# Moving GpSimd's subtractions to VectorE in a fused attention and two-MLP kernel, and pinning one more weight chunk in VectorE's order

## The chip, the cores and the metric

The kernel runs on one core of a Trainium2 chip. The metric is the device time of one execution in microseconds. Three runs of the kernel before gave 616.75 us (median), 614.03 and 618.17.

## The reference

Causal attention over 2 batches, 12 heads, 448 positions and a head size of 64 gives 896 tokens of width 768. They go through two MLPs, all in fp32:

```
x = attention(q, k, v)                       # softmax, masked above the diagonal
h = x @ w_in;  g = 0 | (h+1)^2/4 | h         # 768 -> 2048, piecewise
y = g @ w_out                                # 2048 -> 768
u = silu(y @ w_gate) * (y @ w_val)           # 768 -> 1536, twice
out = u @ w_out2                             # 1536 -> 768
```

## The kernel before, in words

**Splitting.** TensorE reads operands rounded to `fp32r`. Each fp32 operand x is therefore split into a high part (a rounded copy, made by ScalarE) and a low part (x minus the high part, a subtraction). Each product is three matmuls: high times high, high times low, low times high (`mm3`, L83 to L86, and `add`, L717). A low part of weights is named `wl` (L212), `vl` (L256, half of a chunk of `val`) or `ol` (L244, the last projection); of y it is `yl`, of the sums of y `tl` (both L96). The high parts are `wh`, `vh`, `oh`, `yh`, `th`.

**Narrowing.** The weights come from HBM as raw 64-bit words (`wraw`) and are made into 32-bit floats (`wt`) by three VectorE instructions each, `narrow`: L102, L105, L108. A second, independent chain narrows other weights ahead of time in small pieces (`araw`, `at`) and stores them to HBM (`n<-at`, a DMA issued on ScalarE's queue, L140); they come back later as `wraw<-n`.

**Stages.** Attention for both halves of the tokens, with the first products of h beside it (to 146 us); the rest of h (to 231); y, six column blocks d of three weight pieces each, 96 matmuls a block (231 to 350.5); gate and val, twelve chunks f; the last projection, 21 groups of 18 matmuls (534.6 on). Chunks 0, 1, 10 and 11 use `eight`: eight products of 9 matmuls, 72 in all. Chunks 2 to 9 use `seven`: Strassen-like sums of y (`T1` to `T4`, raw form `traw`) and of the weights (`ws`, split into `sh` and `sl`) save one product of eight, 63 matmuls a chunk. There ScalarE copies partial results out of PSUM (`one`, `two`, `three`, `five`, L745 to L758) before TensorE may add to the same bank again.

**Buffers.** Weight halves stand in `WBUFS = 4` rotating buffers, so the split of weight i waits until TensorE has used weight i - 4. Raw words have two buffers, narrowed words (`wt`) two.

**Order.** The Tile layer places each engine's instructions by its own plan of times and priorities; at run time every engine works strictly in that order and waits where an operand is missing. In `narrowing`, a flag `pin` calls `tc.keep_in_program_order` on the first instruction, so that the planner may not bring it ahead of what stands before it in the program. `PIN0, PIN1` bound the weights of gate and val for which the flag is set: numbers 0 and 1 are gate and val of chunk 0, 2 and 3 those of chunk 1.

**The splits of y** stand in the program behind the last block of y: twelve `yh`/`yl` pairs (two token halves g, six blocks c; `yl0_3` is g = 0, c = 3), then the last three `traw`, then four `th`/`tl`. The first product of chunk 0 needs `yl0_0`, the sixteenth matmul `yh0_5`, the 37th `yh1_0`.

Of the kernel before, what the change touches and what calls it, by code (L numbers as in the profile page):

```python
# [8 lines left out]
F32 = mybir.dt.float32  # L9
# [4 lines left out]
ALU = mybir.AluOpType  # L14
# [13 lines left out]
HALF = DM // 2  # L28
# [7 lines left out]
EARLY = WBUFS + STAY  # L36
MASK = -1.0e9 * 8.0
BF16 = mybir.dt.bfloat16
LOW_V = 9
NORM_P = 0  # L40
TURN0 = "A"
TURN1 = "A"
# [1 line left out]
NORM1 = "V"  # L44
SEVEN = (2, 3, 4, 5, 6, 7, 8, 9)
TICK8 = (1, 2)
PIN0, PIN1 = 4, 28
APART = (3, 4, 6, 8, 9)
PART, PART_BUFS = 384, 2
TERMS = (("Z11", "W11"), ("Z21", "W12"), ("T1", "S1"), ("T2", "S2"), ("Z22", "S4"), ("T3", "S3"), ("T4", "W22"))  # L50
# [16 lines left out]
def fused_kernel(ctx: ExitStack, tc: tile.TileContext, qk, v, w_in, w_out, w_gv, w_o2, out):  # L67
    nc = tc.nc
# [74 lines left out]
    class Weights:  # L143
# [36 lines left out]
        def operations(self):  # L180
            for at, (kind, i, src, n) in enumerate(self.seq):
# [20 lines left out]
                if f in SEVEN and i < I_O2:  # L202
# [8 lines left out]
                nc.scalar.copy(out=wh[:, :n], in_=t)  # L211
                (nc.vector if i < LOW_V else nc.gpsimd).tensor_tensor(  # L212
                    out=wl[:, :n], in0=t, in1=wh[:, :n].bitcast(F32), op=ALU.subtract,
# [5 lines left out]
        def term(self, at, i):  # L219

            k, p = divmod(i - I_O2, OUT_PAIRS)
            name = TERMS[k][1]
            if k < 2:
                t = quads[0].tile([128, WB], I32, name=f"{name}_{p}")
                yield from self.narrowing(at, self.raw.pop(("op", i)), t, False)
                quad[name, p] = t.bitcast(F32)
            elif k == 2 and p == 0:
                for q in range(OUT_PAIRS):
                    for low in ("W21", "W22"):
                        quad[low, q] = quads[1].tile([128, WB], F32, name=f"{low}_{q}")  # L230
                        nc.sync.dma_start(out=quad[low, q], in_=stored[low, q])
            made = {
                "S1": ("W21", "W22", "W21", ALU.add), "S2": ("S1", "W11", "S1", ALU.subtract),
                "S4": ("W12", "S2", "W12", ALU.subtract), "S3": ("W22", "S2", "W11", ALU.subtract),
            }
            if name in made:
                a, b, home, op = made[name]
                nc.vector.tensor_tensor(out=quad[home, p], in0=quad[a, p], in1=quad[b, p], op=op)
                quad[name, p] = quad[home, p]
                yield  # L240
            wh = wp.tile([128, WB], F32R, tag="wh", name="oh")
            wl = wp.tile([128, WB], F32R, tag="wl", name="ol")
            nc.scalar.copy(out=wh, in_=quad[name, p])
            (nc.vector if k else nc.gpsimd).tensor_tensor(  # L244
                out=wl, in0=quad[name, p], in1=wh.bitcast(F32), op=ALU.subtract)
            self.got[i] = wh, wl
            self.ready = i + 1
            yield

        def sums(self, i, gate, val):  # L250

            g, v = ([x[:, k * HALF:(k + 1) * HALF] for k in range(2)] for x in (gate, val))
            wh = wp.tile([128, WB], F32R, tag="wh", name="vh")
            wl = wp.tile([128, WB], F32R, tag="wl", name="vl")
            nc.scalar.copy(out=wh[:, :HALF], in_=v[1])
            nc.gpsimd.tensor_tensor(out=wl[:, :HALF], in0=v[1], in1=wh[:, :HALF].bitcast(F32), op=ALU.subtract)  # L256
            t = sums_p.tile([128, 4 * HALF], F32, tag="s", name="ws", bufs=1)
            sh = sums_p.tile([128, 3 * HALF], F32R, tag="sh", name="sh")
            sl = sums_p.tile([128, 3 * HALF], F32R, tag="sl", name="sl")
            s1, s2, s3, s4 = (t[:, k * HALF:(k + 1) * HALF] for k in range(4))  # L260
            nc.vector.tensor_tensor(out=s1, in0=v[0], in1=v[1], op=ALU.add)
            nc.vector.tensor_tensor(out=s2, in0=s1, in1=g[0], op=ALU.subtract)
            yield
            nc.vector.tensor_tensor(out=s4, in0=g[1], in1=s2, op=ALU.subtract)
            nc.vector.tensor_tensor(out=s3, in0=g[0], in1=v[0], op=ALU.subtract)
            yield
            for hi, lo, x in ((sh[:, :WB], sl[:, :WB], t[:, :WB]), (sh[:, WB:], sl[:, WB:], s3),
                              (wh[:, HALF:], wl[:, HALF:], s4)):
                nc.scalar.copy(out=hi, in_=x)
                (nc.vector if S_LOW == "V" else nc.gpsimd).tensor_tensor(  # L270
                    out=lo, in0=x, in1=hi.bitcast(F32), op=ALU.subtract)
                if x is not s4:
                    yield
            self.got[i] = wh, wl, sh, sl
            self.ready = i + 1
            yield
# [25 lines left out]
    for i, (src, n) in enumerate(srcs):  # L302
# [3 lines left out]
        if i >= I_O2:  # L306
            k, p = divmod(i - I_O2, OUT_PAIRS)
# [61 lines left out]
    with ExitStack() as ph:  # L369
# [158 lines left out]
        def zeros(n):  # L528
# [10 lines left out]
            out=mask_b[:C, :], in_=mask_b[:C, :], compare_op=ALU.is_ge, fill=MASK,  # L539
# [115 lines left out]
    for d in range(KC):  # L655
        pss = [bank() for _ in range(2)]
        for i, (a, b) in enumerate(OUT_CUTS):
            wi = I_Y + 3 * d + i
            wh, wl = W.get(wi)
# [78 lines left out]
    def seven(f, ws):  # L738
# [10 lines left out]
        nc.vector.tensor_tensor(out=b, in0=b, in1=one, op=ALU.add)  # L749
        W.tick(1)  # L750
        add(a, sums, HALF, sums_of(1), False, True)
        nc.scalar.copy(out=two, in_=a)
        W.tick(1)
        add(c, sums, 0, sums_of(0), True, True)
        nc.scalar.copy(out=five, in_=c)
        W.tick(1)
        add(a, sums, 2 * HALF, sums_of(2), False, True)
        nc.scalar.copy(out=three, in_=a)  # L758
        W.tick(1)
# [71 lines left out]
    for k in range(len(TERMS)):  # L831
# [3 lines left out]
        for p in range(OUT_PAIRS):  # L835
# [6 lines left out]
            for c in range(6):  # L842
                sl = slice(c * 128, (c + 1) * 128)
                for e, (a, b) in enumerate(((0, 0), (0, 1), (1, 0))):
                    nc.tensor.matmul(  # L845
                        out=ps, lhsT=w[a][:, sl], rhs=rows[c][b],
# [59 lines left out]
```

## Time and profile before

| | |
|---|---|
| median of three runs | 616.75 us |
| profiled execution | 616.38 us |
| its span in the trace | 614.6 us |
| TensorE busy | 589.0 us, 96% |
| VectorE busy | 483.4 us, 79% |
| ScalarE busy | 261.5 us, 43% |
| GpSimd busy | 92.5 us, 15% |

The profiled execution lasts 1.8 us longer than its span, which begins with the first and ends with the last instruction recorded. PE is TensorE, DVE is VectorE, ACT is ScalarE, POOL is GpSimd. A group's idle time is the time its engine stood before these instructions, with what ended it.

### The profile page before, as it was taken

The page shows a single profiled execution, that of the slowest core. Times are in us where ns is not written, and L with a number is a line of the kernel's source. Part 1 is how long each engine was busy: PE and PEld are TensorE (multiplying, and loading weights), DVE is VectorE, ACT ScalarE, POOL GpSimd, SP SyncE. Part 2 cuts the span into 40 slices and gives each one's busy share as a digit, 9 for nine tenths or more (in the row PEclk, how much of TensorE's full clock was granted, in tenths as well). Part 3 has the DMA queues.
Part 4 walks back from the last instruction along what each step waited for, and adds up shares of the span by engine and source line. Part 5 has one row for each costly group of instructions (what it writes and reads, how often), then busy time and mean ns, then how long its engine had stood idle before and what let it go on. Part 6 is the DMA issues. An engine that isn't in the chain of part 4 may idle for free.

```text
span 614.6 us, 8587 instructions
## 1 busy us (share of the span) xinstructions
PE 589.0 (96%) x3185; PEld 502.6 (82%) x3190; DVE 483.4 (79%) x827; ACT 261.5 (43%) x530; POOL 92.5 (15%) x59
## 2 busy tenths in 40 slices
PE   9999999999999999999999879899878999999997
PEld 5766666668999999999999769788777989999997
DVE  3999999854966776756988799758997479999970
ACT  3987766653434432111210363343344342346531
POOL 0000000001302222212421322212231024200000
PEclk9999999999999999999999979999999999999999
DMA  7575554300421227577697422312434134711021
GB/s 259 166 216 187 162 165 134 104 2 1 136 69 51 86 86 218 175 259 248 188 286 255 131 99 103 129 53 98 134 102 129 52 103 135 260 68 45 1 76 60
DMA packets 26009, 80.38 MB, mean 131 GB/s; under 512 B 2928, under 2 KB 10672, under 8 KB 25968
## 3 DMA queue, kind: packets, MB, share of 16 engines
q1 hardware_dynamic: 21792, 73.54, 37.4%
q10 hardware_dynamic: 4176, 6.29, 2.7%
q8 instruction: 25, 0.41, 0.3%
q14 instruction: 16, 0.13, 0.1%
HBM read 70.78 MB, written 9.04 MB: 130 GB/s over the span
## 4 chain that ended last, share of the span: by engine, by line
PE 52%; DVE 29%; issue 8%; DMA 7%; ACT 2%; POOL 1%; ACTq 0%; DVEq 0%; POOLq 0%
PE mm L84 19%; PE mm L717 13%; PE mm L845 12%; DVE wt L105 4%; DMA araw<-w_gv 4%; DVE wt L108 3%; DVE s L425 3%; DVE wt L102 3%; DVE p L463 2%; PE mm L86 2%; DMA wraw<-w_gv 2%; PE s L84 1%; DVE yl L96 1%; DVE sl L270 1%; PE mm L530 1%
## 5 line engine op out<-in xcount | busy, mean ns | idle before, releaser
L212 POOL TENSOR_TENSOR wl<-wt,wh 128x768 fp32r<-128x768 f32 (+1 forms) x36 | 67.5, 1877 | 376.7 <-ACT wh L211 362.1
L211 ACT CAST wh<-wt 128x768 fp32r<-128x768 f32 (+1 forms) x45 | 36.4, 808 | 118.4 <-DVE wt L108 30.2
L84 PE MATMUL mm<-gh,wh 128*128 128x448 f32 x192 | 70.7, 368 | 0.0
L84 PE MATMUL mm<-gl,wh 128*128 128x448 f32 x192 | 70.7, 368 | 0.0
L84 PE MATMUL mm<-gh,wl 128*128 128x448 f32 x192 | 70.7, 368 | 0.0
L84 PE MATMUL mm<-xh,wh 128*128 128x448 f32 x165 | 62.9, 381 | 2.3 <-DVE q L345 2.3
L717 PE MATMUL mm<-yl,wh 128*128 128x448 f32 x144 | 53.9, 374 | 6.4 <-DVE yl L96 6.4
L108 DVE SCALAR_TENSOR_TENSOR wt<-wraw,wt 128x768 int32<-128x768 int32 (+1 forms) x51 | 54.8, 1075 | 0.7
L439 ACT ACTIVATE p<-s,mx 112x112 f32<-112x112 f32 (+3 forms) x96 | 46.3, 495 | 20.3 <-DVE mx L427 14.8
L717 PE MATMUL mm<-yh,wl 128*128 128x448 f32 x144 | 53.6, 372 | 0.0
L717 PE MATMUL mm<-yh,wh 128*128 128x448 f32 x144 | 53.4, 371 | 0.0
L102 DVE TENSOR_SCALAR wt<-wraw 128x768 int32<-128x768 int32 (+1 forms) x51 | 33.0, 647 | 24.1 <-POOL wl L212 22.4
L84 PE MATMUL mm<-xl,wh 128*128 128x448 f32 x138 | 50.8, 368 | 0.0
L84 PE MATMUL mm<-xh,wl 128*128 128x448 f32 x138 | 50.8, 368 | 0.0
L105 DVE SCALAR_TENSOR_TENSOR wt<-wraw,wt 128x768 int32<-128x768 int32 (+1 forms) x51 | 49.4, 969 | 0.8
L845 PE MATMUL mm<-ul,oh 128*128 128x448 f32 x126 | 46.0, 365 | 0.0
L845 PE MATMUL mm<-uh,oh 128*128 128x448 f32 x126 | 46.0, 365 | 0.0
L845 PE MATMUL mm<-uh,ol 128*128 128x448 f32 x126 | 46.0, 365 | 0.0
L425 DVE TENSOR_REDUCE s<-s 112x2 f32<-112x224 f32 (+3 forms) x48 | 35.3, 742 | 7.3 <-PE s L86 7.2
L84 PEld LDWEIGHTS mm<-gl,wh 128*128 128x128 f32 x192 | 36.0, 188 | 3.7
L84 PEld LDWEIGHTS mm<-gh,wl 128*128 128x128 f32 x192 | 36.0, 188 | 3.7
L84 PEld LDWEIGHTS mm<-gh,wh 128*128 128x128 f32 x192 | 36.0, 188 | 3.5
(142 smaller groups left out, 1365.1 us busy)
## 6 DMA issues: line engine op xcount, KB each, us to landing
wraw<-w_in SPq DMA_DIRECT2D x16, 768.0 KB, 4.5
wraw<-w_gv SPq DMA_DIRECT2D x14, 768.0 KB, 4.4
wraw<-w_out SPq DMA_DIRECT2D x12, 768.0 KB, 4.8
araw<-w_gv SPq DMA_DIRECT2D x20, 384.0 KB, 5.4
wraw<-w_o SPq DMA_DIRECT2D x9, 768.0 KB, 4.2
n<-at ACTq DMA_DIRECT2D x26, 192.0 KB, 5.1
qk_t<-qk SPq DMA_DIRECT2D x12, 336.0 KB, 3.1
wraw<-n SPq DMA_DIRECT2D x5, 768.0 KB, 4.2
```

Source lines behind the costliest of these rows:

```text
L84: return product(*args, **kw)
L86: return tc.keep_in_program_order(product(*args, **kw))
L102: yield nc.vector.tensor_scalar(out=t, in0=w[:, :, 1], scalar1=3, scalar2=0x3FFFFFF8, op0=ALU.logical_shift_left, op1=ALU.bitwise_and,)
L105: yield nc.vector.scalar_tensor_tensor(out=t, in0=w[:, :, 1], scalar=-0x40000000, in1=t, op0=ALU.bitwise_and, op1=ALU.bitwise_or,)
L108: yield nc.vector.scalar_tensor_tensor(out=t, in0=w[:, :, 0], scalar=29, in1=t, op0=ALU.logical_shift_right, op1=ALU.bitwise_or,)
L211: nc.scalar.copy(out=wh[:, :n], in_=t)
L212: (nc.vector if i < LOW_V else nc.gpsimd).tensor_tensor(out=wl[:, :n], in0=t, in1=wh[:, :n].bitcast(F32), op=ALU.subtract,)
L425: nc.vector.tensor_reduce(out=mx[:, i], in_=s[:C, :, off:off + w], axis=AX.X, op=ALU.max)
L439: nc.scalar.activation(out=p[:, h, off:off + w], in_=s[:C, h, off:off + w], func=AF.Exp, bias=mx[:, i, h:h + 1], scale=0.125, accum_out=sm ...
L463: nc.vector.tensor_scalar(out=ph, in0=ph, scalar1=r, scalar2=None, op0=ALU.mult)
L717: nc.tensor.matmul(out=ps[:, :N], lhsT=w[a][:, sl], rhs=rows[c][b], start=(first and c == i == 0), stop=(last and c == i == 2), skip_group ...
L845: nc.tensor.matmul(out=ps, lhsT=w[a][:, sl], rhs=rows[c][b], start=(not more and c == e == 0), stop=(c == 5 and e == 2), skip_group_check= ...
```

## The change

All 52 subtractions of weights that GpSimd did are done by VectorE: 41 of L212 (35 of 128x768, six of 128x512), eight of L256 (128x384), three of L244 (128x768). GpSimd keeps only the set-up of constants. `PIN0` goes from 4 to 2, which sets the flag for gate and val of chunk 1 as well.

```diff
-LOW_V = 9
+LOW_V = 999
...
-PIN0, PIN1 = 4, 28
+PIN0, PIN1 = 2, 28
...
-            (nc.vector if k else nc.gpsimd).tensor_tensor(
+            nc.vector.tensor_tensor(
                 out=wl, in0=quad[name, p], in1=wh.bitcast(F32), op=ALU.subtract)
...
             nc.scalar.copy(out=wh[:, :HALF], in_=v[1])
-            nc.gpsimd.tensor_tensor(out=wl[:, :HALF], in0=v[1], in1=wh[:, :HALF].bitcast(F32), op=ALU.subtract)
+            nc.vector.tensor_tensor(out=wl[:, :HALF], in0=v[1], in1=wh[:, :HALF].bitcast(F32), op=ALU.subtract)
```

`LOW_V` is the weight number below which L212 runs on VectorE. TensorE's order is the same in both kernels; the planner changes the others.

VectorE at the end of y, before the change. `wt_3534` and `wt_3570` are gate and val of chunk 1, `wt_3480` is val of chunk 0, and `traw` are sums of y of block 4:

```order
L678 TENSOR_TENSOR traw_2594<-mm_3267,traw_2594 128x448
L679 TENSOR_TENSOR traw_2595<-mm_3267,yraw_2593 128x448
L680 TENSOR_TENSOR traw_2595<-mm_3266,traw_2594 128x448
L102 TENSOR_SCALAR wt_3534<-wraw_3417 128x768
L105 SCALAR_TENSOR_TENSOR wt_3534<-wraw_3417,wt_3534 128x768
L108 SCALAR_TENSOR_TENSOR wt_3534<-wraw_3417,wt_3534 128x768
L102 TENSOR_SCALAR wt_3570<-wraw_3484 128x768
L105 SCALAR_TENSOR_TENSOR wt_3570<-wraw_3484,wt_3570 128x768
L108 SCALAR_TENSOR_TENSOR wt_3570<-wraw_3484,wt_3570 128x768
L96 TENSOR_TENSOR yl0_0_3597<-yraw_2592,yh0_0_3596 128x448
L96 TENSOR_TENSOR yl0_1_3601<-yraw_2592,yh0_1_3600 128x448
```

The same place in the changed kernel (the `traw` of block 4 now stand three instructions of `at` before this piece):

```order
L102 TENSOR_SCALAR wt_3534<-wraw_3417 128x768
L105 SCALAR_TENSOR_TENSOR wt_3534<-wraw_3417,wt_3534 128x768
L108 SCALAR_TENSOR_TENSOR wt_3534<-wraw_3417,wt_3534 128x768
L212 TENSOR_TENSOR wl_3487<-wt_3480,wh_3486 128x768
L96 TENSOR_TENSOR yl0_0_3597<-yraw_2592,yh0_0_3596 128x448
L96 TENSOR_TENSOR yl0_1_3601<-yraw_2592,yh0_1_3600 128x448
L96 TENSOR_TENSOR yl0_2_3605<-yraw_2592,yh0_2_3604 128x448
L96 TENSOR_TENSOR yl0_3_3609<-yraw_2592,yh0_3_3608 128x448
L212 TENSOR_TENSOR wl_3541<-wt_3534,wh_3540 128x768
L102 TENSOR_SCALAR wt_3570<-wraw_3484 128x768
L96 TENSOR_TENSOR yl0_4_3613<-yraw_2592,yh0_4_3612 128x448
L105 SCALAR_TENSOR_TENSOR wt_3570<-wraw_3484,wt_3570 128x768
```

Narrowing of chunk 1's gate still stands ahead of the splits of y; that of val now stands between `yl0_3` and `yl1_0`, and the low parts of weights stand among them. Narrowing of `wt_3480` (val of chunk 0), which stood right ahead of the first piece shown and behind all `at` pieces, now stands ahead of the last two of them.

ScalarE in the first `seven` chunk, before the change. `wh_3993` is the high part of the gate weights of chunk 4, whose raw words come by DMA:

```order
L745 COPY one_3868<-mm_3865 128x448
L211 CAST wh_3993<-wraw_3969 128x768
L724 ACTIVATE sg_3960<-mm_3866 128x448
L752 COPY two_3869<-mm_3865 128x448
L755 COPY five_3871<-mm_3867 128x448
```

And in the changed kernel (`o0` is a DMA issue):

```order
L745 COPY one_3868<-mm_3865 128x448
L188 DMA o0_3989<-wt_3949 128x768
L724 ACTIVATE sg_3960<-mm_3866 128x448
L752 COPY two_3869<-mm_3865 128x448
L211 CAST wh_3993<-wraw_3969 128x768
L755 COPY five_3871<-mm_3867 128x448
```

The cast moved from ahead of `two` to behind it, ahead of `five`.

ScalarE in block 4 and 5 of y, before the change: the casts `wh_3317` and `wh_3377` (second and third piece of block 5) stand behind these stores of the `at` chain.

```order
L140 DMA n20_3347<-at_3323 128x384
L140 DMA n20_3347<-at_3349 128x384
L140 DMA n22_3424<-at_3396 128x384
L211 CAST wh_3317<-wt_3311 128x768
L140 DMA n22_3424<-at_3426 128x384
L140 DMA n24_3492<-at_3458 128x384
L141 DMA n24_3492<-at_3494 128x384
L211 CAST wh_3377<-wt_3371 128x512
```

And in the changed kernel:

```order
L140 DMA n16_3213<-at_3288 128x384
L211 CAST wh_3317<-wt_3311 128x768
L140 DMA n20_3347<-at_3323 128x384
L140 DMA n20_3347<-at_3349 128x384
L211 CAST wh_3377<-wt_3371 128x512
L140 DMA n22_3424<-at_3396 128x384
```

Each of the two casts has moved ahead of three or four stores.

## Rows read from the trace of the kernel before

**Rows 1.** The page: span, and busy time by engine (us, share, instructions).
```profile
span 614.6 us, 8587 instructions
PE 589.0 (96%) x3185; PEld 502.6 (82%) x3190; DVE 483.4 (79%) x827; ACT 261.5 (43%) x530; POOL 92.5 (15%) x59
```

**Rows 2.** Stretches: length, busy of PE, PEld, DVE, ACT, POOL; clock; DMA.
```profile
231.00:350.50 119.50, 119.50 (x580) 108.50 (x579) 86.52 (x139) 21.54 (x35) 30.38 (x17) 1.00 0.72 226
356.60:361.00 4.40, 4.37 (x12) 3.84 (x13) 4.40 (x6) 2.04 (x3) 2.27 (x1) 0.50 0.55 179
374.30:504.30 130.00, 118.91 (x573) 106.44 (x572) 98.76 (x130) 49.90 (x92) 27.76 (x18) 1.00 0.32 107
504.30:534.60 30.30, 30.30 (x151) 28.09 (x150) 28.13 (x27) 9.25 (x13) 11.20 (x5) 1.00 0.47 158
534.60:612.00 77.40, 76.61 (x379) 70.66 (x377) 61.94 (x63) 35.67 (x42) 0.00 (x0) 1.00 0.17 63
```

**Rows 3.** What TensorE waited for: us in total, times, longest.
```profile
PE mm L717 <- ACT two L752: 6.4, 4, 2.6
PE mm L717 <- DVE yl L96: 6.4, 2, 5.8
PE mm L717 <- ACT three L758: 3.3, 3, 2.0
```

**Rows 4.** Timeline of TensorE at chunk 0's first, 2nd, 17th, 19th matmul: start, duration.
```profile
350.49 0.37 PE L717 MATMUL mm<-yh,wh 128*128 128x448 f32 x1
356.63 0.74 PE L717 MATMUL mm<-yl,wh 128*128 128x448 f32 x1 [5.78 <-DVE yl L96]
...
362.56 0.47 PE L717 MATMUL mm<-yl,wh 128*128 128x448 f32 x1 [0.60 <-DVE yl L96]
...
363.07 0.37 PE L717 MATMUL mm<-yh,wh 128*128 128x448 f32 x1
```

**Rows 5.** Timeline of VectorE at the end of y.
```profile
342.65 2.17 DVE L102 TENSOR_SCALAR wt<-wraw 128x768 int32<-128x768 int32 x1 [3.12 <-POOL wl L212]
...
348.33 1.78 DVE L102 TENSOR_SCALAR wt<-wraw 128x768 int32<-128x768 int32 x1
...
351.14 0.96 DVE L108 SCALAR_TENSOR_TENSOR wt<-wraw,wt 128x768 int32<-128x768 int32 x1
352.01 0.55 DVE L102 TENSOR_SCALAR wt<-wraw 128x768 int32<-128x768 int32 x1
...
353.59 2.45 DVE L108 SCALAR_TENSOR_TENSOR wt<-wraw,wt 128x768 int32<-128x768 int32 x1
355.96 6.00 DVE L96 TENSOR_TENSOR yl<-yraw,yh 128x448 fp32r<-128x448 f32 x8
```

**Rows 6.** Timeline of GpSimd at the end of y.
```profile
347.83 1.86 POOL L212 TENSOR_TENSOR wl<-wt,wh 128x768 fp32r<-128x768 f32 x1 [3.42 <-ACT wh L211]
353.11 2.11 POOL L212 TENSOR_TENSOR wl<-wt,wh 128x768 fp32r<-128x768 f32 x1 [3.42 <-ACT wh L211]
```

**Rows 7.** Timeline of ScalarE at the end of y.
```profile
347.66 1.97 ACT L95 CAST yh<-yraw 128x448 fp32r<-128x448 f32 x4
352.20 0.83 ACT L211 CAST wh<-wt 128x768 fp32r<-128x768 f32 x1 [2.58 <-DVE wt L108]
```

**Rows 8.** VectorE's groups by shape: count, busy us, mean ns, idle before.
```profile
L212 DVE TENSOR_TENSOR wl<-wt,wh 128x768 fp32r<-128x768 f32 x9 | 8.5, 943 | 0.0
L265 DVE TENSOR_TENSOR ws<-wraw 128x384 f32<-128x384 f32 x5 | 2.7, 549 | 0.0
```

**Rows 9.** Timeline of ScalarE: casts that waited, in y and in a seven chunk.
```profile
266.63 0.84 ACT L211 CAST wh<-wt 128x768 fp32r<-128x768 f32 x1 [14.03 <-DMA n<-at]
397.62 0.83 ACT L211 CAST wh<-wraw 128x768 fp32r<-128x768 f32 x1 [3.96 <-DMA wraw<-n]
```

## The prediction

> **What bounds the kernel now.** I read the page's busy times first, then the stretches by stage, then what TensorE waited for, and last the timelines around its longest wait. The page names VectorE, not GpSimd, as the second busiest engine: 483.4 us of 614.6 [rows 1]. The stretches show that TensorE sets the pace: it is busy without a gap in y (580 matmuls in 119.5 us, 0.206 us each) and nearly so from 504.3 us on [rows 2]. What it loses stands in two places: the start of chunk 0, 6.4 us behind `yl`, and the stage of gate and val, where between 374.3 and 504.3 us it is busy for 118.9 us of 130, so idle for 11.1, mostly behind ScalarE's copies `two` and `three` [rows 2, 3]. Only these two can pay for a change on VectorE; a busy share saved elsewhere buys nothing.
>
> The first place is dearer than its wait. The second matmul of chunk 0 comes 5.78 us late, at 356.63; the 2nd to 13th then run at a granted clock of 0.50, the lower of the two levels (1.2 instead of 2.4 GHz), 4.4 us for twelve; the 17th waits 0.60 more; the 19th starts at 363.07 [rows 2, 4]. Without a gap it would start at 350.49 + 18 x 0.206 = 354.2. So this boundary costs **8.9 us**.
>
> Why is `yl` late? ScalarE has the first four `yh` from 347.66 on [rows 7]. VectorE, from 342.65 on, makes val of chunk 0, then `traw`, then gate and val of chunk 1, and only then, at 355.96, the first `yl` [rows 5]. It began late, after 3.12 us behind GpSimd's low part, whose operand buffer it wanted. And it was slowed: the same L102 took 0.55 us alone and 2.17 and 1.78 beside GpSimd, L108 0.96 and 2.45 [rows 5, 6]: 1.62, 1.23 and 1.49 us too much, 4.3 in all.
>
> **The change part by part.**
>
> *Price of the moved work.* A 128x768 low part takes 0.943 us on VectorE, one of 128x384 0.549 (another subtraction of that shape); one of 128x512 lies between them [rows 8]. 38 x 0.943 + 6 x 0.75 + 8 x 0.549 = 44.7 us more for VectorE. GpSimd's 92.5 us go, and with them the slowing: 1.2 to 1.6 us for each large one beside which VectorE works, so 46 to 61 us if all 38 were such, nothing for those that met an idle VectorE. Its total could end between 467 and 528 us; I take about the 483 of now. What counts is where.
>
> The Trainium skill (SBUF — State Buffer, Who interferes with whom) states that of a VectorE instruction with two SBUF inputs or in a 2-port mode and a GpSimd instruction the later one is blocked fully until the first ends. The L108 that began 0.48 us behind GpSimd's start and ended 0.82 us after its end agrees [rows 5, 6]. By that rule a moved large low part frees up to 1.86 us for 0.943, and the seven stage would gain about 1 us more than I take below.
>
> *In y.* 18 low parts, at most 17 us, join VectorE's 86.5 of 119.5 us [rows 2]: it has room. A low part is held until TensorE frees its buffer, four weights back, so weights are ready some three pieces ahead; TensorE does not wait. Zero; bounds are the rivals' below.
>
> *End of y.* Block 5 takes 96 x 0.206 = 19.8 us and begins at 330.7; its first piece (36 matmuls) is used up at 338.1, the second at 345.5. In the new order the low part of chunk 0's val (`wl_3487`) stands last before `yl0_0` and waits for the first of these: 338.1 + 0.83 (a cast [rows 7]) + 0.94 = 339.9; four `yl` of about 0.61 follow, to 342.4. The last `at` piece and the gate of chunk 1 stand ahead; they may make this 2 us later, and it is wanted at 350.7. Then `wl_3541` waits for the second piece: 345.5 + 0.83 + 0.94 = 347.3; L102 0.55, `yl0_4` 0.61, L105 0.96, `yl0_5` 0.61 (350.0, wanted by the 17th matmul at 353.8), L108 0.96, `yl1_0` and `yl1_1` (352.2, wanted from 358.1), `wl_3577`, four more `yl` (355.7). None is late. I take 8.6 of the 8.9 us and leave 0.3 for semaphores. Bounds: nothing gained, if an operand comes 9 us later than this; 8.9.
>
> *In the seven stage.* 18 of GpSimd's instructions lie here [rows 2], ten large and eight half ones: VectorE takes 10 x 0.943 + 8 x 0.549 = 13.8 us and loses about 18 (the large ones at 1.4, the middle of [rows 5], the half ones at an estimated 0.5). Its 98.8 us of 130 become about 95 of 119 to 130. One stall can be followed: ScalarE's cast at 397.62 waited 3.96 us for a DMA, with `two` behind it, and TensorE lost 2.6, the longest in its list [rows 3, 9]. In the new order that cast stands behind `two` and ahead of `five`; the DMA starts when VectorE is done with the buffer, as before, so `five` loses about 0.9 instead: 1.7 us gained. Of the other 8.5 us I take 1.8, since VectorE becomes quicker but stays nearly full. Together 3.5. Bounds: all 11.1 gained; or 13.8 lost, if the added work all lands on TensorE.
>
> *Behind it.* From 504.3 to 534.6 VectorE is busy for 28.1 of 30.3 us and TensorE throughout [rows 2]; five low parts (4.7 us) come for five that slowed it by about 7. Zero; bounds 2.3 lost, nothing gained. In the last projection GpSimd did nothing: zero. Before 231 us a few low parts join an unstalled TensorE: zero.
>
> *Sum.* 616.38 - 8.6 - 3.5 = **604.3 us**. The profiled execution lies 0.4 under the median of 616.75; I leave that in the range.
>
> **The rivals.**
>
> 1. *VectorE becomes the bound in the seven stage.* In a chunk that also narrows its weights VectorE has about as much to do as TensorE's 63 x 0.206 = 13.0 us; each low part now also stands in its queue behind a ScalarE cast. If the slowing is not given back there, 98.8 + 13.8 = 112.6 us stand against 118.9, and I would expect the stalls to grow by about half, 5 us: 616.4 - 8.6 + 5 = 612.8. For it: 95% filling. Against: the slowing is in the rows. The Trainium skill (Perfetto Trace Analysis, Optimizing Scalar/DVE Operations) speaks for this rival: it advises offloading from a saturated VectorE to Scalar or GpSimd, which this change undoes, though it adds that the two share a port and that offloading between them might not help.
>
> 2. *The splits come late all the same.* Chunk 1's gate is still narrowed ahead of `yl0_0`, so the pin does only half of what it is said to do, and three narrowing steps and two low parts (2.5 + 1.9 us) stand among the `yl`. If stores and DMAs of the `at` chain put VectorE 5 us behind my times, half the boundary returns: 616.4 - 4.4 - 3.5 = 608.5.
>
> 3. *Slower: VectorE stands behind ScalarE's stores in y.* A cast waited 14.03 us there behind the `at` chain's stores [rows 9]; GpSimd could wait for it at no cost, VectorE cannot, since it narrows the next weights and feeds the same stores. The low part of chunk 0's val, GpSimd's at 347.83, ended at 349.7, 4.5 us before its use at 350.5 + 18 x 0.206 = 354.2 [rows 6]; with that lead a hold decides once it exceeds 4.5 us, one of 14 costs 9.5, and a VectorE so late loses the boundary too: 616.4 + 9.5 = 625.9. Against: the new order puts casts ahead of three or four more stores than before, and by the buffers the lead can be 20 us.
>
> 4. *The seven stage's stalls go altogether.* 616.4 - 8.6 - 11.1 = 596.7, if nothing but GpSimd's slowing made them.
>
> **How the numbers follow.** My forecast 0.58, rival 1 0.16, rival 2 0.13, rival 3 0.07, rival 4 0.06. A measurement of this kernel tells about 1% (6 us) from no change. The forecast's own spread, by the bounds of the seven stage, is 600 to 608; the range reaches to rivals 1 and 2 and part of the way to 4: 599.5 to 612.5. Faster by over 1% (under 610.6): forecast, rivals 2 and 4 and a third of rival 1, 0.80; within 1%: the rest of rival 1 and part of 2 and 3, 0.14; slower 0.06.
>
> **What would show it.** Right, if TensorE has no gap over 1 us at the first products of chunk 0 and no clock of 0.50 behind it; if the first `yl` starts before 346 us; if L102 stays near 0.55 us everywhere; and if the stage from there to the last projection has under 11 us of idle TensorE. Wrong, if TensorE waits within y, for `wl` now made on VectorE; if the `yl` start later than 350; or if its waits behind `two`, `five` and `three` add up to more than before, which would make VectorE's filling, not its slowing, the cause.

## The result, and the profile after

| | before | changed |
|---|---|---|
| median of the runs | 617.46 us (614.03 to 619.41, 4 runs) | **597.11 us** (589.48 to 597.52, 4 runs) |
| ratio, 95% interval | | **0.9647** (0.9558 to 0.9736) |
| profiled execution: time, span | 616.38, 614.6 us | 597.38, 595.6 us |

A ratio leaves out executions that lie over 1.5% above the kernel's fastest (among the kernels below, one of e4's, 597.50 us).

The kernel became faster by 3.5%, more than forecast: 604.3 us was predicted, and 597.11 lies 2.4 us below the range (599.5 to 612.5). It is the time that the fourth rival gave (596.7), to which I had put a chance of 0.06; that the two agree to 0.4 us is luck, since executions of this kernel lie up to 8 us apart.

The profiled execution is 19.0 us shorter. TensorE's idle time explains 17.5 of them: 614.6 - 589.0 = 25.6 us before [rows 1], 595.6 - 587.5 = 8.1 now. The other 1.5 are busy time: twelve matmuls at the lower clock behind the gap at chunk 0 had taken 4.4 us [rows 2], where twelve at 0.206 take 2.5, and TensorE's pace differs between the two executions as well (last section). The span and the engines' busy time on the page after, with share and instructions:

```profile
span 595.6 us, 8508 instructions
PE 587.5 (99%) x3190; PEld 501.3 (84%) x3190; DVE 482.3 (81%) x879; ACT 264.2 (44%) x530; POOL 0.9 (0%) x7
```

VectorE has 44.7 us more work by my count and a total that is 1.1 us smaller: about 46 us of slowing went with GpSimd's work. All that TensorE still waits for lies ahead of 142 us (from the waits of the kernel after; engine, tile, line, releaser: us in total, times, longest); [rows 3] are gone:

```profile
PE mm L84 <- DVE q L345: 2.3, 4, 1.3
PE mm L530 <- DVE half_b L535: 1.2, 1, 1.2
PE o L84 <- ACT pt L483: 0.9, 1, 0.9
PE s L84 <- ACT p L439: 0.2, 1, 0.2
```

The stretches after, which answer to [rows 2] (width, busy time and instructions of each engine, granted clock of TensorE, DMA share, GB/s):

```profile
core 0: us, PE busy (x) PEld busy (x) DVE busy (x) ACT busy (x) POOL busy (x), PEclk, DMA share, GB/s
231.00:350.40 119.40, 119.40 (x579) 108.45 (x578) 94.91 (x166) 25.17 (x41) 0.00 (x0) 1.00 0.72 232
350.40:356.60 6.20, 6.20 (x32) 5.63 (x31) 5.95 (x12) 5.51 (x6) 0.00 (x0) 1.00 0.38 128
365.30:484.00 118.70, 118.70 (x576) 107.79 (x576) 92.98 (x148) 51.79 (x93) 0.00 (x0) 1.00 0.36 117
484.30:514.50 30.20, 30.20 (x148) 27.43 (x147) 26.72 (x35) 8.68 (x12) 0.00 (x0) 1.00 0.52 174
```

The stage of seven products (both stretches also hold chunk 1, of eight products) takes 118.7 us instead of 130, and TensorE is never idle in it. VectorE's *share* of the stage is no smaller than before: 92.98 of 118.7 is 78%, 98.76 of 130 was 76% [rows 2]. What differs is that some of its instructions were long. By form in the stage, before (line, engine, operation, tiles, shapes, count | busy us, mean ns | idle before):

```profile
L105 DVE SCALAR_TENSOR_TENSOR wt<-wraw,wt 128x768 int32<-128x768 int32 x10 | 12.0, 1198 | 0.2
...
L270 DVE TENSOR_TENSOR vl<-ws,vh 128x384 fp32r<-128x384 f32 x8 | 8.5, 1057 | 0.9 <-ACT vh L269 0.9
L102 DVE TENSOR_SCALAR wt<-wraw 128x768 int32<-128x768 int32 x10 | 8.2, 825 | 1.3 <-DMA wraw<-w_gv 1.3
...
L766 DVE TENSOR_TENSOR five<-five,three 128x448 f32<-128x448 f32 x8 | 7.5, 934 | 12.5 <-ACT three L758 12.5
...
L749 DVE TENSOR_TENSOR mm<-mm,one 128x448 f32<-128x448 f32 x8 | 5.0, 627 | 3.8 <-PE mm L717 3.8
```

and after (a view that ends at 480 us, 4 us before the stage does):

```profile
L105 DVE SCALAR_TENSOR_TENSOR wt<-wraw,wt 128x768 int32<-128x768 int32 x10 | 9.5, 952 | 0.1
...
L102 DVE TENSOR_SCALAR wt<-wraw 128x768 int32<-128x768 int32 x10 | 5.5, 553 | 0.0
L749 DVE TENSOR_TENSOR mm<-mm,one 128x448 f32<-128x448 f32 x8 | 5.0, 631 | 4.7 <-PE mm L717 2.9 <-ACT wh L211 1.8
...
L270 DVE TENSOR_TENSOR vl<-ws,vh 128x384 fp32r<-128x384 f32 x8 | 4.4, 550 | 0.0
...
L766 DVE TENSOR_TENSOR five<-five,three 128x448 f32<-128x448 f32 x7 | 4.4, 622 | 11.3 <-ACT three L758 11.3
```

The differences times the counts, with those of the other forms of the same view, add up to 18.5 us before. L749, which reads one operand from PSUM, was not slowed (627 against 631 ns), though four of its eight lay beside a GpSimd subtraction. Of the instructions that read two operands from SBUF, and of the first narrowing step, those were slowed that began while a GpSimd subtraction ran: 18 in the stage before, which hold all of the 18.5 us. Seven that had begun when a GpSimd subtraction did kept their time (an L105 its 0.96 us, for one). The Trainium skill (SBUF — State Buffer, Who interferes with whom) says the same: one SBUF input outside the two-port modes does not contend with GpSimd, two do.

At chunk 0 the answer to [rows 4] is a row without a gap (TensorE's timeline after: start, duration; an idle time before it would stand in brackets), 0.206 us apart:

```profile
350.04 0.37 PE L84 MATMUL mm<-gh,wl 128*128 128x448 f32 x1
350.24 0.37 PE L717 MATMUL mm<-yh,wh 128*128 128x448 f32 x1
350.45 0.37 PE L717 MATMUL mm<-yl,wh 128*128 128x448 f32 x1
350.66 0.37 PE L717 MATMUL mm<-yh,wl 128*128 128x448 f32 x1
```

because VectorE, where [rows 5] had the first `yl` at 355.96, starts them at 341.56 (its timeline after):

```profile
340.69 0.95 DVE L212 TENSOR_TENSOR wl<-wt,wh 128x768 fp32r<-128x768 f32 x1
341.56 2.22 DVE L96 TENSOR_TENSOR yl<-yraw,yh 128x448 fp32r<-128x448 f32 x4
346.19 0.96 DVE L212 TENSOR_TENSOR wl<-wt,wh 128x768 fp32r<-128x768 f32 x1 [2.41 <-ACT wh L211]
```

### The profile page after: what moved, and what is told of

It is laid out like the page before. It is cut to its first block, busy times and chain, and to the rows that moved or that the text cites. A ratio compares the mean times of both kernels' runs of the same rounds, so it can differ in the third digit from the quotient of the medians.

```text
span 595.6 us, 8508 instructions
## 1 busy us (share of the span) xinstructions
PE 587.5 (99%) x3190; PEld 501.3 (84%) x3190; DVE 482.3 (81%) x879; ACT 264.2 (44%) x530; POOL 0.9 (0%) x7
## 4 chain that ended last, share of the span: by engine, by line
PE 84%; DVE 13%; ACT 2%; DMA 1%; issue 0%; ACTq 0%
PE mm L84 35%; PE mm L717 27%; PE mm L845 13%; DVE s L425 3%; DVE p L463 2%; PE mm L86 2%; PE s L84 1%; DVE wt L108 1%; PE mm L530 1%; DVE wt L105 1%; ACT p L439 1%; DVE wl L212 1%; DMA wraw<-w_in 1%; PE t L86 1%; PE s L86 1%; DVE wt L102 1%
## 5 line engine op out<-in xcount | busy, mean ns | idle before, releaser
L439 ACT ACTIVATE p<-s,mx 112x112 f32<-112x112 f32 (+3 forms) x96 | 46.4, 497 | 19.9 <-DVE mx L427 14.4
L212 DVE TENSOR_TENSOR wl<-wt,wh 128x768 fp32r<-128x768 f32 (+1 forms) x45 | 41.2, 916 | 11.6 <-ACT wh L211 11.3
L105 DVE SCALAR_TENSOR_TENSOR wt<-wraw,wt 128x768 int32<-128x768 int32 (+1 forms) x51 | 46.9, 920 | 0.7
L108 DVE SCALAR_TENSOR_TENSOR wt<-wraw,wt 128x768 int32<-128x768 int32 (+1 forms) x51 | 46.9, 920 | 0.4
L84 PEld LDWEIGHTS mm<-xh,wh 128*128 128x128 f32 x165 | 31.0, 188 | 6.2 <-DVE q L345 3.4
```

Source lines behind the costliest of these rows:

```text
L84: return product(*args, **kw)
L105: yield nc.vector.scalar_tensor_tensor(out=t, in0=w[:, :, 1], scalar=-0x40000000, in1=t, op0=ALU.bitwise_and, op1=ALU.bitwise_or,)
L108: yield nc.vector.scalar_tensor_tensor(out=t, in0=w[:, :, 0], scalar=29, in1=t, op0=ALU.logical_shift_right, op1=ALU.bitwise_or,)
L212: (nc.vector if i < LOW_V else nc.gpsimd).tensor_tensor(out=wl[:, :n], in0=t, in1=wh[:, :n].bitcast(F32), op=ALU.subtract,)
L439: nc.scalar.activation(out=p[:, h, off:off + w], in_=s[:C, h, off:off + w], func=AF.Exp, bias=mx[:, i, h:h + 1], scale=0.125, accum_out=sm ...
```

## The experiments

TensorE's idle time below is the sum of its waits in the stage of seven products and at chunk 0; of before it was 11.1 and 6.4 us. It tells kernels apart better than the medians do, since the pace of TensorE itself varies by up to 10 us between executions (last section). "VectorE" is its busy time in the stage and the length of that stage, from the first matmul of chunk 1 to the last of chunk 9; before it was 99.3 of 131.1 us.

| kernel | median us | ratio to before, 95% | idle, stage | idle, chunk 0 | VectorE |
|---|---|---|---|---|---|
| changed | 597.11 | 0.965 (0.956 to 0.974) | 0 | 0 | 93.4 of 119.1 |
| e1: before, stage's low parts moved | 604.5 | 0.977 (0.973 to 0.982) | 2.4 | 8.1 | 93.1 of 121.1 |
| e2: changed, stage's given back | 607.17 | 0.981 (0.977 to 0.985) | 10.2 | 0 | 99.5 of 131.6 |
| e4: changed, no pin | 594.77 | 0.958 (0.951 to 0.965) | 0 | 0 | 92.3 of 119.0 |
| e5: changed, GpSimd busy at other places | 597.84 | 0.966 (0.962 to 0.970) | 2.9 | 0 | 99.2 of 120.8 |
| e6: changed, GpSimd busy at the old places | 607.07 | 0.981 (0.977 to 0.984) | 9.7 | 0 | 109.8 of 130.4 |
| e7: changed, sums twice | 590.65 | 0.956 (0.953 to 0.959) | 1.0 | 0 | 107.3 of 118.4 |
| e8: changed, low parts twice | 592.34 | 0.957 (0.952 to 0.962) | 0 | 0 | 103.2 of 118.6 |
| e9: changed, chunks 0 and 1 given back | 592.65 | 0.957 (0.954 to 0.961) | 2.2 | 0 | 92.8 of 119.2 |
| e10: sums twice, order kept | 609.6 | 0.986 (0.983 to 0.990) | 9.2 | 0 | 110.4 of 133.5 |
| e11: e6 in the order of e7 | 601.7 | 0.976 (0.971 to 0.981) | 7.4 | 0 | 111.9 of 126.5 |
| e12: changed, y's low parts given back | 599.87 | 0.971 (0.966 to 0.976) | 0.5 | 4.0 | 95.7 of 119.8 |

**Are the two gains separate? e1 and e2.**

```diff
 # e1, from before (the low part in sums likewise)
-                (nc.vector if i < LOW_V else nc.gpsimd).tensor_tensor(
+                (nc.vector if i < LOW_V or i >= I_GV + 4 else nc.gpsimd).tensor_tensor(
 # e2, from the changed kernel (the low part in sums back on gpsimd)
-                (nc.vector if i < LOW_V else nc.gpsimd).tensor_tensor(
+                (nc.vector if i < I_GV + 4 else nc.gpsimd).tensor_tensor(
```

> The kernel before, with only the low parts of gate and val from chunk 2 on moved to VectorE; those of y's end and of chunks 0 and 1 stay on GpSimd, the pin as before. Theory A (GpSimd's subtractions slow VectorE's instructions beside them, ScalarE's casts come late, TensorE stands behind ScalarE's copies): each half of the gain is local. The 11.1 us of TensorE's idle time in the stage of seven products go, the 8.9 us at the start of chunk 0 stay: 616.4 - 11.1 = about 605 us, TensorE idle under 1.5 us in the stage. Rival B (the late start of chunk 0 is handed on, and the stage's stalls are its echo): the stage still loses 7 us or more, 612 us or above. Rival C (VectorE stays nearly full, as the prediction had it): 3.5 of 11.1 go, about 613 us.

> The changed kernel, with the low parts of gate and val from chunk 2 on given back to GpSimd; y's end and chunks 0 and 1 as changed. Theory A: the start of chunk 0 stays without a gap, and the stage loses its 11 us again: 597.4 + 11.1 = about 608 us, with VectorE's narrowing back at 0.65 us or more for the first step and 1.0 us or more for the others inside the stage. Rival B (stalls inherited from chunk 0): under 600 us. Rival C: 597.4 + 3.5 = about 601 us.

Both nearly as theory A had it: the stage's stalls follow the stage's low parts (2.4 and 10.2 us of idle), the gap at chunk 0 stays in e1 and stays away in e2. Rival B, the echo of a late start, falls, and so does rival C. e1 keeps 2.4 us where under 1.5 were expected: one stall with a cause of its own, the wait for a refill of [rows 9] (see the next section).

**GpSimd beside an order that is not touched: e5 and e6.**

```diff
 # e5: started by one and five, from and to a scratch tile
+        nc.gpsimd.tensor_copy(out=scratch[:, :8], in_=t[:, :8])
+        nc.gpsimd.tensor_tensor(out=scratch[:, :n], in0=scratch[:, :n], in1=scratch[:, :n], op=ALU.subtract)
 # e6: behind each cast of gate, and of val (half as wide) likewise
+                    nc.gpsimd.tensor_tensor(out=scratch, in0=t, in1=wh.bitcast(F32), op=ALU.subtract)
```

> The changed kernel, its order on TensorE, VectorE, ScalarE and the queues untouched, plus dummy subtractions on GpSimd that nobody waits for: in each chunk of seven products one of 128x768 and one of 128x384, from and to a scratch tile in SBUF, each started when ScalarE has written one and five. This puts GpSimd's work back beside VectorE without any wait on GpSimd and without a change of order. Theory A: VectorE's instructions become slower as before (18 us in the stage: 98.8 - (93.0 - 12.5)), now on top of the low parts: VectorE near 110 of 119 us in the stage and TensorE stalls again by 8 to 20 us, 605 to 617 us. Rival D (the stalls came from the old order, and from waits on GpSimd): 597 to 599 us, no stall over 1 us.

> The changed kernel, its order on TensorE, VectorE, ScalarE and the queues untouched, plus the old GpSimd subtractions of the stage of seven products at their old places, done a second time into a scratch tile that nobody reads: one of 128x768 per gate, one of 128x384 per val, each behind the same cast of ScalarE and with the same operands as before. Theory A (beside GpSimd's subtraction, those VectorE instructions become longer on which ScalarE's casts wait, and so TensorE): VectorE grows by 15 to 25 us in the stage, from 93 to 108 to 118, the first narrowing step, the sums and vl are the ones that grow, and TensorE loses 8 us or more in the stage behind two and three: 605 us or more. Rival D (the old order made the stalls, the slowing lies in VectorE's slack): under 2 us of idle TensorE in the stage, 597 to 599 us.

e5 missed: GpSimd is busy for 31.8 us in the stage, but VectorE grows by only 5.8 and TensorE loses 2.9. The dummies begin when ScalarE has written `one` and `five`, and it is mostly low parts, behind the casts, that lie beside them there (L212 grew to 1076 and 1079 ns, L256 to 747 and 760; L108 grew to 1055, the narrowing's other steps and the sums not at all). Nor is it true that nobody waits: VectorE's sum of `five` and `three` waited 4.6 us for the dummy that reads `five`. e6 puts them where the old ones were, and nearly all of the stage's loss is back, 9.7 us, in the very order of the changed kernel, with VectorE nowhere waiting for GpSimd. So the stalls need neither the old order nor a wait on GpSimd. One of them can be read in full. First GpSimd, then VectorE, ScalarE and TensorE in e6 (their timelines; in e6 L265 is the second sum of the weights, L272 a cast of sums):

```profile
390.95 2.65 POOL L216 TENSOR_TENSOR scratch<-wraw,wh 128x768 f32<-128x768 f32 x1 [5.25 <-ACT wh L211]
...
391.82 2.20 DVE L265 TENSOR_TENSOR ws<-ws,wraw 128x384 f32<-128x384 f32 x1
...
394.12 0.83 ACT L272 CAST sh<-ws 128x768 fp32r<-128x768 f32 x1 [2.87 <-DVE ws L265]
394.86 0.53 ACT L762 COPY three<-mm 128x448 f32<-128x448 f32 x1
...
395.44 0.47 PE L721 MATMUL mm<-th,vh 128*128 128x448 f32 x1 [2.04 <-ACT three L762]
```

and the same three in the changed kernel:

```profile
387.95 0.55 DVE L262 TENSOR_TENSOR ws<-ws,wraw 128x384 f32<-128x384 f32 x1
...
389.34 0.83 ACT L269 CAST sh<-ws 128x768 fp32r<-128x768 f32 x1 [1.16 <-PE mm L717]
390.08 0.53 ACT L758 COPY three<-mm 128x448 f32<-128x448 f32 x1
```

The sum takes 0.55 us alone and 2.20 beside GpSimd, ending 0.42 after GpSimd does. ScalarE works in order, and its next instruction is the cast of that sum; `three`, whose product is done, stands behind the cast; TensorE stands behind `three`. The rule of the Trainium skill that I set against the trace ahead of the result (same page and section: the later one is blocked until the first ends) agrees with this row. e6 isn't the slowing alone: its GpSimd also holds the raw weights longer, and the waits for the DMA that refills them (ScalarE's and VectorE's) are 4.7 us in e6 and 2.0 after.

**Is it VectorE's filling? e7 and e8.**

```diff
 # e7: each of the four sums twice, as here
             nc.vector.tensor_tensor(out=s2, in0=s1, in1=g[0], op=ALU.subtract)
+            nc.vector.tensor_tensor(out=s2, in0=s1, in1=g[0], op=ALU.subtract)
 # e8: each low part of gate and val twice, as here
             nc.vector.tensor_tensor(out=wl[:, :HALF], in0=v[1], in1=wh[:, :HALF].bitcast(F32), op=ALU.subtract)
+            nc.vector.tensor_tensor(out=wl[:, :HALF], in0=v[1], in1=wh[:, :HALF].bitcast(F32), op=ALU.subtract)
```

> The changed kernel with VectorE's four sums of the weights done twice in each chunk of seven products (the second writes the same values): 32 x 0.55 = 17.6 us more for VectorE, about what GpSimd's slowing cost before (18.5 us), ahead of the casts that ScalarE makes of these sums, and GpSimd idle. Some order on VectorE and ScalarE moves with it. If time on VectorE ahead of ScalarE's casts is what counted, whatever its cause (theory A in its wide form): TensorE idle for 5 to 11 us in the stage, 602 to 608 us. If only GpSimd's presence does harm: under 2 us, 597 to 599 us. If VectorE were nearly full, as the prediction argued (93 + 17.6 = 110.6 of 118.7): 12 us or more.

> The changed kernel with VectorE's low parts of gate and val done twice in each chunk of seven products: 8 x (0.95 + 0.55) = 12 us more for VectorE, behind the casts instead of ahead of them. Some order on VectorE and ScalarE moves with it. Theory A with room on VectorE (26 us idle in the stage): no stall of TensorE over 1 us, 597 to 599 us. The prediction's argument (nearly full): about half of the 12 us show up on TensorE, 602 us or more.

Filling is not the cause. VectorE is busy for 107.3 of 118.4 us in e7, 91%, and TensorE waits 1.0 us in all, far less than in e6, where VectorE has about as much to do in a longer stage. But e7's order was made with the longer sums counted in: ScalarE's casts of them stand later among its copies. The order of e8, where 9.8 us more cost nothing, was made anew likewise.

**The same time, in an order that doesn't count it: e10; and the slowing in an order that counts more: e11.**

```diff
 # e10, from e7: the order of the changed kernel, as dependencies without a wait, for TensorE, ScalarE, VectorE
+        chain = []
+        for at in order:
+            chain.append(own[at])
+            if own[at].name in again:
+                chain.append(again[own[at].name])
+        for left, right in zip(chain, chain[1:]):
+            tc.add_manual_dep(right, left.name, ...)
 # e11, from e6: the same with the order of e7
```

> The changed kernel with VectorE's four sums done twice in each chunk of seven products, as in e7 (17.6 us more for VectorE, GpSimd idle), but with the order of TensorE, VectorE and ScalarE from chunk 0 on written out as the changed kernel has it, each second sum right behind its first. In e7 the order had been made anew with the longer times counted in. Theory A, narrow form (time on VectorE that the order doesn't count makes the sums late, the casts of the sums stand ahead of two and three on ScalarE, which works in order; GpSimd is one source of such time): TensorE stalls return, 5 to 12 us behind two and three, 602 to 609 us. Rival E (only where GpSimd strikes matters: the narrowing steps, vl and five; VectorE has room for 17.6 us at the sums in any order): under 2 us of idle TensorE in the stage, 590 to 598 us.

> e6 (the changed kernel with the old GpSimd subtractions of the stage done a second time at their old places, which cost it 9.7 us of idle TensorE in the stage), with the order of TensorE, VectorE and ScalarE from chunk 0 on written out as e7 had it, where the sums were counted twice as long. VectorE's instructions are those of e6. Theory A, narrow form: the same slowing, but ScalarE's copies now stand ahead of more of the late casts: TensorE idle for 1 to 6 us in the stage instead of 9.7, 598 to 604 us. Rival E (the slowing itself is too much in any order): 9 us or more, 606 us or more.

e10 has the work of e7 and stalls like e6: 9.2 us (4.8 of it behind `five`), GpSimd idle. At the same place as above, ScalarE and TensorE in e10 (L292 the cast of sums, L272 all sums):

```profile
394.62 0.83 ACT L292 CAST sh<-ws 128x768 fp32r<-128x768 f32 x1 [3.05 <-DVE ws L272]
395.35 0.53 ACT L781 COPY three<-mm 128x448 f32<-128x448 f32 x1
...
395.93 0.47 PE L740 MATMUL mm<-th,vh 128*128 128x448 f32 x1 [2.23 <-ACT three L781]
```

So time on VectorE ahead of ScalarE's casts costs TensorE time if the order was made without it, whether GpSimd causes it or work of VectorE's own. The counterpart for time behind the casts, e8's work in the order of the changed kernel, was not run. e10 lost more time than it idled; its granted clock is 0.96 in the stage. e11 lies between the two expectations: 7.4 us of idle remain of 9.7. The waits behind `two` and `three` fall from 7.6 to 2.3 us; new ones behind `sh` and `sl`, the products' own operands, take 4.4. A better order hides a part of the slowing and not most of it.

**Which part cured chunk 0? e4, e9 and e12.**

```diff
 # e4
-PIN0, PIN1 = 2, 28
+PIN0, PIN1 = 4, 28
 # e9
+                (nc.gpsimd if I_GV <= i < I_GV + 4 else nc.vector).tensor_tensor(
 # e12
+                (nc.gpsimd if I_Y <= i < I_GV else nc.vector).tensor_tensor(
```

> The changed kernel with the pin back at 4: chunk 1's gate is narrowed ahead of the first four yl, everything else as changed. The prediction's second rival gave the missing pin 4.4 us. By durations of the changed kernel's trace: wl_3487 done at 341.6, three narrowing steps (2.5 us) to 344.1, four yl to 346.3, wl_3541 347.3, yl0_4 347.9, yl0_5 about 350: TensorE reaches chunk 0 at 350.2, so theory A (low parts are what matters) says no gap over 0.5 us and 597 to 599 us; the rival (the order of the pin is half of the gain at chunk 0) says 601 to 602 us with 4 us of gap at chunk 0.

> The changed kernel with only the low parts of gate and val of chunks 0 and 1 given back to GpSimd; those of y's weights stay on VectorE, the pin stays at 2. In the resulting order the narrowing of chunk 1's gate stands ahead of the first yl again. Theory A: beside GpSimd's subtractions of chunk 0's weights the narrowing steps take up to 2.2 us instead of 0.55 and wait for its buffer: the first yl is 3 to 6 us later than in the changed kernel (341.6), so done near the time of need (350.2), and the others late: a gap of 2 to 6 us at chunk 0, 600 to 604 us. Rival (the y stage's low parts made VectorE late, not chunk 0's): no gap over 0.5 us, 597 to 599 us.

> The changed kernel with only the low parts of y's weights given back to GpSimd; those of gate and val stay on VectorE. In the order chunk 1's gate stays behind the first four yl. If VectorE is as late at the end of y as before (val of chunk 0 begun at 342.65), then three steps of narrowing and a low part (3.4 us, up to 5 beside GpSimd) come first, the first four yl stand at 346 to 348 and are done by 350.4, yl0_5 near 353: wanted at 350.2 and 353.8, so a gap of 0 to 1 us at chunk 0 and 597 to 599 us (theory: the order at the end of y and the slowing in y are each cure enough). Rival (the slowing in y alone makes the boundary's cost): a gap of 4 to 9 us, 602 to 606 us.

e4 has no gap: without the pin chunk 1's val is narrowed ahead of the first `yl` again (the expectations of e4, e9 and e12 say the gate, which stands ahead of them in all), but they start at 342.28, in time for 349.8. e9 missed: one L108 took 2.54 us beside GpSimd, and in its order, too, chunk 1's val stands ahead of the first `yl`, yet these start at 341.68 and there is no gap (its 2.2 us in the stage are the stall of [rows 9], as in e1). e12 missed the other way: the gap is back with y's low parts, though the pin is in and chunk 0's are on VectorE (TensorE in e12):

```profile
348.73 0.36 PE L717 MATMUL mm<-yh,wh 128*128 128x448 f32 x1
353.06 0.74 PE L717 MATMUL mm<-yl,wh 128*128 128x448 f32 x1 [3.97 <-DVE yl L96]
353.60 0.57 PE L717 MATMUL mm<-yh,wl 128*128 128x448 f32 x1
```

and its VectorE is late because in y it waits for the buffers that GpSimd's low parts hold (its waits from 200 to 362 us):

```profile
DVE wt L102 <- POOL wl L212: 21.0, 12, 2.5
```

So y's own low parts made most of the boundary's cost: the first `yl` start at 341.56 in the changed kernel, at 352.39 in e12 and at 355.96 before, so they bring 10.8 of the 14.4 us between the two kernels. With y's low parts on VectorE, neither the pin nor those of chunks 0 and 1 are needed (e4, e9). The other 3.6 us I did not divide among them; put alone into the kernel before, the pin changes no instruction's place. e4, which is simpler, is not told apart from the changed kernel: 594.77 against 597.11 us, within the intervals.

**The changed kernel again.** No edit.

> The changed kernel once more, beside the others on one chip. Its four timed executions lay at 589.5 and at 596.8 to 597.5 us with the same granted clock; kernels without stalls have since shown 0.202 or 0.206 us per matmul in the same stage. Expected: every execution near one of the two values, none between 591 and 596 us, if the pitch holds over a whole execution; a spread between them if it changes within one.

It gave 588.45, 598.06, 598.36 and 598.61 us, near the two values and none between. Kernels without a stall lie between them all the same (e4's 592.79 us, e8's 594.80): the pace can change within an execution (last section).

## Why the prediction was wrong in size and right in direction

- *What bounds the kernel*: right. TensorE sets the pace, and only chunk 0 and the stage of seven products could pay: 17.5 us of idle went, 6.4 and 11.1.
- *Price of the moved work*: right. A low part takes 951 ns on VectorE; the slowing given back, 46 us, lies at the lower end of 46 to 61, and the total came out at 482.3 where I took about 483.
- *In y*: zero was right for TensorE, which doesn't wait there for a `wl`. But I treated the low parts of y as a price without a return; e12 and e9 show that moving them is what cured chunk 0.
- *End of y*: right in size. I took 8.6 of 8.9 us and all 8.9 went; the times came within 1.7 us (first `yl` done by 342.4, measured 343.8; last 355.7, measured 354.8). Of the two causes that I read off [rows 5], the wait for GpSimd's buffer and the slowing, the wait is the larger: in e12 VectorE waits 21.0 us for such buffers, its three narrowing steps are slowed by some 4.4 us over y (1110 instead of 953 ns for L105, for one), none of the last before the first `yl` is, and a gap is there. The order that I followed in detail was not needed (e4).
- ***In the seven stage*: the step that failed.** I took 3.5 of 11.1 us, and all 11.1 went. It failed at "Of the other 8.5 us I take 1.8, since VectorE becomes quicker but stays nearly full": all 8.5 went. VectorE's time came as forecast, 93.4 of 119.1 us (78%) for "about 95 of 119 to 130". The inference from it was wrong: at 91% in e7 TensorE hardly waits, and at 83% in e10 it does. What counts is whether a sum or a narrowed weight is late for the cast that ScalarE has next, with `two`, `three` or `five` behind it. The low parts that VectorE took over stand behind the casts that they need, and the order was made with them; of the 18.5 us of slowing some 10 stood ahead of casts, those of the sums (4.8) and of the narrowing (5.2). The view to read was not VectorE's busy share but ScalarE's waits, in the stage before (engine, tile, line, releaser: us in total, times, longest):

```profile
ACT wh L211 <- DVE wt L108: 11.0, 5, 4.2
ACT vh L255 <- DVE wt L108: 10.7, 4, 4.3
...
ACT sh L269 <- DVE ws L262: 7.3, 4, 3.0
...
ACT sh L269 <- DVE ws L265: 5.4, 2, 3.9
```

  and after:

```profile
ACT wh L211 <- DVE wt L108: 4.4, 4, 3.2
...
ACT sh L269 <- DVE ws L262: 2.7, 4, 1.4
...
ACT sh L269 <- DVE ws L265: 1.0, 2, 0.6
...
ACT vh L255 <- DVE wt L108: 0.5, 1, 0.5
```

  34.4 us there, 8.6 now. They show where the loss comes from and not its size: such waits are 22.1 us in e6 and 27.9 in e10, for 9.7 and 9.2 us of idle TensorE, and 14.6 in e7 for 1.0.

  The one stall that I did follow, ScalarE's cast behind a DMA [rows 9], was not GpSimd's. In e1 GpSimd has nothing to do in the stage, the cast stands ahead of `two` as before, and the stall of 2.4 us is there (ScalarE):

```profile
397.81 0.83 ACT L211 CAST wh<-wraw 128x768 fp32r<-128x768 f32 x1 [4.21 <-DMA wraw<-n]
...
399.38 0.53 ACT L752 COPY two<-mm 128x448 f32<-128x448 f32 x1
```

  e9 has the same with 2.2 us. In the changed kernel the cast stands behind `two`, as I had read it, and costs `five` nothing:

```profile
385.78 0.53 ACT L752 COPY two<-mm 128x448 f32<-128x448 f32 x1 [0.58 <-PE mm L717]
386.21 0.84 ACT L211 CAST wh<-wraw 128x768 fp32r<-128x768 f32 x1
```

  Its refill also came sooner, 4.3 us after its start instead of 5.8 (6.0 in e1, 5.9 in e9); how much each of the two did is not separated. So of the 11.1 us GpSimd's low parts made about 8.7 (e1), and this refill the rest.
- *The range*: its spread, "600 to 608", was not that of the seven stage's bounds, as I wrote. All 11.1 us gained, or 13.8 lost, give 596.7 to 621.6.
- *Behind it*: right, zero.
- *Rivals*: rival 1 (VectorE becomes the bound) is refuted by e7 and e8, and with it the advice of the Trainium skill that I had put beside it (Perfetto Trace Analysis, Optimizing Scalar/DVE Operations) has no hold here; its reservation, that work moved between VectorE and GpSimd might not help since they share a port, agrees with the slowing that the runs show. Rival 2 gave the late splits 4.4 us; they came in time, even without the pin (e4). Rival 3 didn't occur: TensorE has no wait in y. Rival 4, "if nothing but GpSimd's slowing made them", is what happened in the main, with two reservations: the stall of [rows 9] had another cause, and held buffers had a small part (e6).
- *What would show it*: every sign came (no gap at chunk 0, first `yl` before 346, L102 at 0.55, under 11 us idle). They could not tell 3.5 from 11.1.

## What to carry to other kernels

When another engine slows VectorE, don't size the effect by VectorE's busy share; find the slowed instructions, ask which in-order engine has their consumer next, and look at that engine's waits on them. Some 17 us more on VectorE, in an order made without them, cost 9 to 10 us of idle TensorE, whether GpSimd's slowing (e6) or VectorE's own work (e10) was the cause. Where they were counted in when the order was made, 13.9 us cost 1.0 (e7) and 9.8 us nothing (e8). So an order stops being right where engines collide, and taking the collision away can pay although the engine's total stays as it was (483.4 and 482.3 us here).

## What the runs showed of the hardware that I had not expected

- TensorE has two paces at the same granted clock. In the same stretch of time, without a gap, e4's profiled execution did 579 matmuls in 119.4 us and e7's 591, 0.206 and 0.202 us each (stretch 231 to 350.4 of e4, then of e7):

```profile
231.00:350.40 119.40, 119.40 (x579) 108.45 (x578) 97.28 (x170) 25.52 (x43) 0.00 (x0) 1.00 0.73 236
```
```profile
231.00:350.40 119.40, 119.40 (x591) 110.67 (x590) 97.26 (x171) 27.79 (x44) 0.00 (x0) 1.00 0.72 232
```

  Over the 2322 matmuls of this shape such a difference comes to 2322 x 0.004 = 9.3 us, about what lies between the executions of one kernel (the changed kernel again: 588.45, and 598.06 to 598.61 us). It can change within an execution: e12 is at 0.202 ahead of its gap (490 matmuls in the 99.0 us from 231 to 330) and at 0.206 to 0.207 from 359 us on. The kernel before goes the other way in its profiled execution, from 0.206 to 0.202 behind a stall at 394 us, while that of the changed kernel, without a stall, stays at 0.206 to its end; so these two compare at unequal paces. e8 quickens at 451 us without a stall. What sets the pace stays open.
- GpSimd is slowed as well. Its subtraction of 128x768 took 1.49 us on the mean in e5, and 2.35 and 3.16 (by operands) in e6; one took 6.78.
